# Modulation weights in an adaLN decode block: 128 rows of two terms loaded by four transfers of eight rows

## The chip, the cores and the metric

The kernel runs on one core of one Trainium2 chip. The time is the device time of one execution in microseconds (us); lower is better. The core has five engines, each with an instruction stream of its own: TensorE (PE in the profile, with PEld for its weight loads), VectorE (DVE), ScalarE (ACT), GpSimd (POOL) and SyncE (SP). Data moves between HBM and the on-chip memory SBUF through 16 DMA engines. A transfer is issued as one instruction, here nearly always by SP, and its parts run on several DMA engines side by side. SBUF has 128 partitions; a tile is a number of partitions by a number of bytes in each.

## The reference

One decoding step of a transformer block with adaptive layer norm, four sequences (B = 4), width D = 512, float32 throughout:

```
mod = silu(c) @ w_mod                    # c: 4 x 512, w_mod: 512 x (6*512)
sa, ca, ga, sb, cb, gb = mod in six terms of 4 x 512
h = layernorm(x) * (1 + ca) + sa
x = x + ga * attention(h, k_cache, v_cache, wq, wo)   # 32 query heads, 8 KV heads, 4096 keys of 128
h = layernorm(x) * (1 + cb) + sb
x = x + gb * mixer(h, w1, b1, w2, b2)    # 1 -> 1792 -> 1 per channel, GELU between
```

The K and V caches are 4 x 8 heads x 4096 x 128 floats each: 32 pairs (batch, head) of 2 MB of K and 2 MB of V. `w_mod` is 6 MB: six terms of 512 x 512 floats, 1 MB each. The terms are called 0 to 5 here (sa, ca, ga, sb, cb, gb). A term's 512 rows are the contraction; they are laid out as four blocks of 128 rows (k = 0 to 3), one row to a partition.

## The kernel before

All large arrays go through a ring of three SBUF buffers of 32 KB per partition (pool `ring`, tag `kv`). A buffer is filled by one or more transfers issued by SP; SP waits before it issues until the matmuls that read the buffer's former content are done, so the ring sets the order and the earliest time of every load. SP issues in the order of the program text and does not overtake: a transfer that has to wait holds up all later ones. In order: terms 0 and 1 (`wm01`, 2 MB), the small vectors in three transfers of 6, 10 and 112 partitions, `x`, the query weights (two of 4 MB), the first two K blocks (`load_first`), then one transfer of 4 MB per step with the K of pair i+2 and the V of pair i side by side (`load_pair`), and between them the output weights (`load_wo`, four of 2 MB, which stay in SBUF), terms 2 to 4 (`load_wm24`, 3 MB, one ring buffer, issued in step 1 of the main loop) and, close to the end, term 5 (`load_wm5`).

The main loop runs over the pairs 0 to 23. Step i issues the load for pair i+1, computes the scores of pair i+2 (`scores`, L238, eight matmuls of 128x512 that read K), their row maximum (L243), exponentials (L268), the transposes of pair i+1 (L275), the weighted V sums of pair i (`values`, L301) and the output projection (L337) of pair i-1. From step 9 on, the mixer of a finished batch row is worked in beside it (class `Mixer`). Step 2 also computes the modulation terms 2, 3 and 4: `mod(t)` runs 16 matmuls (`modmm`, L223: four row blocks k by four column blocks c), whose stationary operand is `sT8[:, k]`, silu(c) of that row block repeated to 32 columns, and whose moving operand is the term's block `WM[t][:, k, ...]`; the result is copied to `prep` (L614, L616). The last eight pairs follow an order written out by hand (`PLAN`), in which v29.0 or v31.3 stands for a part of the V sums of pair 29 or 31, and the loads of V for pairs 28 to 31 are transfers of their own (`load_v`, L218); that of pair 31 comes in four pieces of 1 MB, 0.5 MB and twice 0.25 MB. The last pair's V sums are L309. After them come the last batch row's residual, layer norm, mixer (L431, L537, L542) and the output.

`silu(c)` is made at the start from 16 columns `cT` of the small vectors: one activation (L119) and four VectorE instructions (L120 to L124), 16 columns wide, the last of them 128.

The lines that the change and the steps of the prediction touch are L54 to L61 (first loads), L119 to L124 (silu), L137 (terms 0 and 1), L190 (`load_pair`), L199 and L200 (`load_wm24`), L206 (`load_wm5`), L218 (`load_v`), L223 (`modmm`), L301 and L309 (V sums).

Of the kernel before, what the change touches and what calls it, by code (L numbers as in the profile page):

```python
# [8 lines left out]
F32 = mybir.dt.float32  # L9
# [6 lines left out]
B, D, HQ, HKV, SK, DH, F = 4, 512, 32, 8, 4096, 128, 1792  # L16
REP = HQ // HKV
NF = F // 128
EPS = 1e-5
P = 128  # L20
NS = B * HKV
NSM = 3 * NF + 16 + 1

# [5 lines left out]


@with_exitstack
def adaln_decode(ctx: ExitStack, tc: tile.TileContext, small, x, wmod, wq, kk, kv, vv, wo, out):
    nc = tc.nc
    pad = ctx.enter_context(tc.tile_pool(name="pad", bufs=1))
    ring = ctx.enter_context(tc.tile_pool(name="ring", bufs=3))
    wos = ctx.enter_context(tc.tile_pool(name="wos", bufs=1))
    cst = ctx.enter_context(tc.tile_pool(name="cst", bufs=1))
    wk = ctx.enter_context(tc.tile_pool(name="wk", bufs=2))  # L40
    up = ctx.enter_context(tc.tile_pool(name="up", bufs=3))
# [5 lines left out]
    mm = nc.tensor.matmul  # L47
    dv = nc.vector

    neg1 = pad.tile([1, 96], F32, name="neg1")[:, 0:1]  # L50
    sm = cst.tile([P, NSM], F32, name="sm")
    xr = wk.tile([P, D], F32, name="xr", tag="yw", bufs=1)[0:B]
    wm01 = ring.tile([P, 2, 4, D], F32, name="wm01", tag="kv")
    nc.sync.dma_start(wm01, wmod[0])  # L54
    for lo, hi in ((0, 6), (6, 16), (16, P)):
        nc.sync.dma_start(sm[lo:hi], small[lo:hi])
    nc.sync.dma_start(xr, x)
# [1 line left out]
    for k in range(0, 4, 2):  # L59
        t = ring.tile([P, 2, HQ * DH], F32, name=f"wq{k}", tag="kv")  # L60
        nc.sync.dma_start(t, wq[k // 2])  # L61
        wqt += [t[:, 0], t[:, 1]]
    w1, b1, w2 = sm[:, 0:NF], sm[:, NF:2 * NF], sm[:, 2 * NF:3 * NF]
    cT = sm[:, 3 * NF:3 * NF + 16]
    b2 = sm[:, 3 * NF + 16:]

    ident = cst.tile([P, P], F32, name="ident")
    make_identity(nc, ident)
# [25 lines left out]
    wo_t = [wo_p[h // 2][:, h % 2] for h in range(HKV)]  # L94
    prep = cst.tile([P, 4, P], F32, name="prep")
    osb = cst.tile([P, B, P], F32, name="osb")
    sT8 = cst.tile([P, 4, B, 8], F32, name="sT8")

    def rsqrt(ve, n, tag, beside=None, out=None, times=None):
        y = wk.tile([n, 1], F32, name="y" + tag)  # L100
# [11 lines left out]
        if times is not None:  # L112
# [2 lines left out]
        dv.scalar_tensor_tensor(y, q, RS3, y, op0=OP.add, op1=OP.mult)  # L115
        return y

    sg = cst.tile([P, 16], F32, name="sg")
    nc.scalar.activation(sg, cT, AF.Exp, scale=-1.0)  # L119
    dv.tensor_scalar(sg, sg, 1.0, None, op0=OP.add)  # L120
    dv.reciprocal(sg, sg)
    sT = cst.tile([P, 4, B], F32, name="sT")
    dv.tensor_mul(sT.rearrange("p k b -> p (k b)"), sg, cT)  # L123
    dv.tensor_copy(sT8.rearrange("p k b r -> p (k b) r"),  # L124
                   sT.rearrange("p k b -> p (k b)").unsqueeze(2).to_broadcast([P, 16, 8]))

    st = wk.tile([B, 6], F32, name="st0")
    dv.bn_stats(st, xr)
# [34 lines left out]
    rows = cst.tile([B, B, 8], F32, name="rows")  # L163
# [7 lines left out]
    KT, VT, WM = {}, {}, {}  # L171

    def slots():
        return ring.tile([P, 2, SK], F32, name="kv", tag="kv")
# [20 lines left out]
        nc.sync.dma_start(wo_p[h // 2], wo[h // 2])  # L195

    def load_wm24():
        w = ring.tile([P, 3, 4, D], F32, name="wm24", tag="kv")
        nc.sync.dma_start(w[:, 0:2], wmod[1])  # L199
        nc.sync.dma_start(w[:, 2], wmod[2][:, 0])  # L200
        for e in range(3):
            WM[2 + e] = w[:, e]

    def load_wm5():
        t = slots().rearrange("p s (k n) -> p (s k) n", n=D)
        nc.sync.dma_start(t[:, 0:4], wmod[2][:, 1])  # L206
        WM[5] = t[:, 0:4]
        return t[:, 4:6]

    def load_key(t, i):  # L210
# [6 lines left out]
        for lo, hi in zip(cuts, cuts[1:]):  # L217
            nc.sync.dma_start(VT[i][:, lo:hi], src[:, lo:hi])  # L218

    def modmm(pm, t, ks=range(4)):  # L220
        for k in ks:
            for c in range(4):
                mm(pm[32 * c:32 * c + 32, :], sT8[:, k].rearrange("p b r -> p (b r)"),  # L223
                   WM[t][:, k, c * P:(c + 1) * P], start=(k == 0), stop=(k == 3))

    def mod(t):
        pm = ps_e.tile([P, P], F32, name=f"pm{t}", tag="e")
        modmm(pm, t)
        return pm
# [348 lines left out]
    for i in range(NS - HKV):  # L578
# [3 lines left out]
        if i == 1:  # L582
            load_wm24()
# [25 lines left out]
        if i == 2:  # L609
            for t in range(2, 5):  # L610
                pm = mod(t)
# [32 lines left out]
    for step in PLAN.split():  # L644
        op, k = step.rstrip("0123456789."), step.lstrip("abcdefghijklmnopqrstuvwxyzABCDEFGHIJKLMNOPQRSTUVWXYZ")
        i, q = (int(n) for n in (k + ".0").split(".")[:2]) if k else (0, 0)
# [19 lines left out]
        elif op == "LV":  # L666
            load_v(slot[:, i % 2], i, cuts.get(i, (0, 32)))
        elif op == "LW":
            spare = load_wm5()
        elif op == "x":  # L670
            mix.expand(spare if mix.n == 6 else None)
        elif op == "f":
            fold_gate(gate, gates[:1])
            del gates[:1]
        elif step == "T":
            nc.scalar.activation(tab, neg1, AF.Exp)
        elif op == "Y":
            pgx = ps_s.tile([P, 8, P], F32, name="pgx", tag="s")
        elif op == "y":
            pc = fold_groups(ps_m, ACC.pop(B - 1), "m")  # L680
        elif op == "E":
            ep = cst.tile([P, P], F32, name="ep")
            residual(ep, pc)
        elif op == "I":
            mm(pgx[:, 4], ident, ep, start=False, stop=False)
        elif step == "T2":
            nc.scalar.activation(tab, neg1, AF.Abs_reciprocal_sqrt)
        elif step == "T3":
            nc.scalar.activation(tab, neg1, AF.Gelu_apprx_tanh)
        elif op == "zs":  # L690
            row.st = stats(pgx[:, 4], B - 1)
        elif op == "zx":
            dv.tensor_copy(XK[:, B - 1], pgx[:, 4])
        elif op == "zw":
            modmm(pgx[:, 0], 5, (0,) if i == 0 else (1, 2, 3))
        elif op == "zb":
            if i == 0:
                py = ps_s.tile([P, 8, P], F32, name="py3", tag="s")
            row.spread(py[:, 4:], (2 * i, 2 * i + 1))
# [35 lines left out]
```

## Time and profile before

| | us |
|---|---|
| median of 3 runs | 389.47 (389.02 to 390.22) |
| span of the profiled execution, first to last instruction | 386.9 |
| DMA queue of SP (q1), share of 16 engines' span | 94.8% |
| PE busy (weight loads apart) | 298.9 |
| VectorE busy | 215.2 |
| ScalarE busy | 108.0 |
| bytes read from HBM | 157.32 MB |

The profiled execution's own time is its span, 386.9 us, and what lies around it before the first and after the last instruction; the runs' median is 2.6 us above the span. A row of the timeline gives the start, the duration, the engine, the line, the operation, the tiles written and read, and in brackets the idle time before it with what ended it. In the answer by windows, each stretch has its busy time per engine, the granted TensorE clock, the mean busy share of the 16 DMA engines (a share of 0.5 is eight engines at work on average) and GB/s. A share slightly above 1 comes from packets that overlap at their edges or reach over the edge of the window.

### The profile page before, as it was taken

How to read it: one execution, taken by the hardware profiler on the slowest of the kernel's cores; microseconds unless marked ns; L12 is line 12 of the kernel's file. 1: busy time of each engine (PE TensorE's matmuls, PEld its weight loads, DVE VectorE, ACT ScalarE, POOL GpSimd, SP SyncE). 2: the span in 40 equal slices, each digit the busy share in tenths (PEclk: the TensorE clock that was granted, in tenths of full speed). 3: DMA queues.
4: the chain of work that ended last, by engine and by line, in shares of the span. 5: the costliest groups of instructions: out<-in, count | busy, mean ns of one | idle time of the engine just before them, and what ended most of it. 6: DMA issues, size and time to landing. Idle time of an engine off the chain costs nothing.

```text
span 386.9 us, 5714 instructions
## 1 busy us (share of the span) xinstructions
PE 298.9 (77%) x2416; PEld 122.4 (32%) x2416; DVE 215.2 (56%) x516; ACT 108.0 (28%) x132; POOL 0.7 (0%) x6
## 2 busy tenths in 40 slices
PE   0765575863966949979888859999988887999984
PEld 0111121231323313334222323443323342444562
DVE  0420351620542524676766644676875579788766
ACT  0101120110110110113567210213783104757356
POOL 0000000000000000000000000000000000000000
PEclk9998875986695775989999985978999998899999
DMA  8999999999999999999999999999999999999910
GB/s 329 430 434 434 415 451 430 410 449 432 418 447 434 430 434 432 434 432 434 426 434 429 434 429 434 434 432 434 425 434 432 434 429 434 422 427 423 404 46 3
DMA packets 7281, 157.70 MB, mean 408 GB/s; under 512 B 964, under 2 KB 980, under 8 KB 1368
## 3 DMA queue, kind: packets, MB, share of 16 engines
q1 hardware_dynamic: 7248, 157.33, 94.8%
q8 instruction: 19, 0.31, 0.3%
q14 instruction: 6, 0.05, 0.0%
q10 hardware_dynamic: 8, 0.00, 0.0%
HBM read 157.32 MB, written 0.01 MB: 407 GB/s over the span
## 4 chain that ended last, share of the span: by engine, by line
DMA 54%; PE 28%; DVE 16%; issue 1%; SPq 1%; ACTq 0%; DVEq 0%
DMA kv<-in_kv 47%; PE s L238 8%; PE pv L301 7%; DMA wq<-in_wq 6%; DVE m L243 3%; DVE p L275 3%; PE pt L324 2%; PE pa L337 2%; PE pb L258 2%; DVE uu L431 1%; DVE mx L252 1%; DVE acc L353 1%; PE qs L152 1%; PE phb L417 1%; PE pve L309 1%
## 5 line engine op out<-in xcount | busy, mean ns | idle before, releaser
L238 PE MATMUL s<-kv,QT 128*32 128x512 f32 x512 | 76.2, 715 | 35.6 <-DMA kv<-in_kv 32.6
L268 ACT ACTIVATE p<-s,nm 128x1024 f32<-128x1024 f32 x32 | 35.6, 1114 | 199.0 <-DVE nm L263 198.9
L243 DVE TENSOR_REDUCE m<-s 128x1 f32<-128x1024 f32 x32 | 39.2, 1224 | 76.1 <-PE s L238 76.0
L301 PE MATMUL pv<-kv,p 128*32 128x512 f32 x496 | 75.0, 684 | 0.4 <-DMA kv<-in_kv 0.4
L275 DVE STREAM_TRANSPOSE p<-p 128x512 f32<-128x512 f32 x64 | 41.9, 687 | 1.7 <-ACT p L268 1.7
L324 PEld LDWEIGHTS pt<-sel,po 128*128 128x128 f32 x250 | 33.6, 208 | 28.7 <-issue 15.6
L238 PEld LDWEIGHTS s<-kv,QT 128*32 128x32 f32 x512 | 16.3, 125 | 81.3 <-DMA kv<-in_kv 45.3
L337 PE MATMUL pa<-wo,oT 128*32 128x512 f32 x240 | 35.3, 663 | 4.3 <-DVE oT L329 4.2
L324 PE MATMUL pt<-sel,po 128*128 128x4 f32 x250 | 36.2, 268 | 1.4 <-DVE po L315 1.4
L315 DVE COPY po<-pv 128x512 f32<-128x512 f32 x31 | 21.4, 689 | 17.0 <-PE pv L301 17.0
L252 DVE TENSOR_REDUCE mx<-pm 1x128 f32<-1x512 f32 x32 | 21.4, 671 | 0.8 <-PE pm L247 0.7
L258 PEld LDWEIGHTS pb<-neg,mx 1*128 1x128 f32 x64 | 10.8, 210 | 32.9 <-DVE mx L252 31.1
L487 ACT ACTIVATE u<-u 128x1024 f32<-128x1024 f32 x20 | 20.4, 1052 | 2.7 <-DVE u L431 2.6
L431 DVE TENSOR_SCALAR u<-hb,wr,sm 128x512 f32<-128x512 f32 x40 | 19.9, 541 | 1.0 <-PE py L442 0.9
L353 DVE TENSOR_TENSOR acc<-acc,pa 128x512 f32<-128x512 f32 x26 | 17.7, 681 | 3.6 <-PE pa L337 3.6
L268 ACT ACT_TABLE_LOAD x11 | 14.1, 1283 | 19.0 <-DVE nm L263 18.9
L137 PE MATMUL s<-wm,sT 128*4 128x512 f32 x16 | 8.4, 684 | 12.2 <-DVE sT L123 12.2
L258 PE MATMUL pb<-neg,mx 1*128 1x1 f32 x64 | 13.5, 278 | 5.3 <-DVE mx L252 5.3
L487 ACT ACT_TABLE_LOAD x13 | 16.7, 1283 | 0.2
L247 PE MATMUL pm<-ident,m 128*1 128x128 f32 x32 | 9.1, 286 | 9.8 <-DVE rl L284 3.8
L301 PEld LDWEIGHTS pv<-kv,p 128*32 128x32 f32 x496 | 14.1, 146 | 8.1 <-issue 2.1
L247 PEld LDWEIGHTS pm<-ident,m 128*1 128x1 f32 x32 | 2.5, 80 | 39.1 <-DVE rl L284 21.0
(144 smaller groups left out, 212.3 us busy)
## 6 DMA issues: line engine op xcount, KB each, us to landing
kv<-in_kv SPq DMA_DIRECT2D x28, 4096.0 KB, 20.8
wq<-in_wq SPq DMA_DIRECT2D x2, 4096.0 KB
wo<-in_wo SPq DMA_DIRECT2D x4, 2048.0 KB
kv<-in_kv SPq DMA_DIRECT2D x4, 2048.0 KB, 18.5
wm<-in_wmod SPq DMA_DIRECT2D x2, 2048.0 KB
kv<-in_kk SPq DMA_DIRECT2D x1, 4096.0 KB
kv<-in_vv SPq DMA_DIRECT2D x3, 1024.0 KB
wm<-in_wmod SPq DMA_DIRECT2D x1, 1024.0 KB
```

What stands on the lines that cost most here:

```text
L238: mm(s[32 * c:32 * c + 32, n * 512:(n + 1) * 512], QT[:, b, h, :], KT[i][:, (n * 4 + c) * 512:(n * 4 + c + 1) * 512], start=True, stop=True)
L243: dv.tensor_reduce(M[i], S[i], axis=AX.X, op=OP.max)
L252: dv.tensor_reduce(mx, M[i].rearrange("o (c r) -> o r c", c=4).unsqueeze(1).to_broadcast([1, 4, 32, 4]), axis=AX.X, op=OP.max)
L258: mm(pb, M[i].rearrange("o c r -> o (c r)"), neg1, start=True, stop=True)
L268: nc.scalar.activation(p, S[i], AF.Exp, bias=M.pop(i), accum_out=l)
L275: dv.transpose(p, p)
L301: mm(PV[i][32 * q:32 * q + 32, :], pT[:, 128 * k:128 * k + 128:4], VT[i][:, 4 * k:4 * k + 4, :].rearrange("p j d -> p (j d)"), start=(k < ...
L324: mm(pt, po[:, c * DH:(c + 1) * DH], sel[:, c, :], start=(c == 0), stop=(c == n - 1))
L337: mm(pa[32 * g:32 * g + 32, :], oT[:, g:g + 1].to_broadcast([P, 32]), wo_t[h][:, g, :], start=True, stop=True)
L353: dv.tensor_add(ACC[b], ACC[b], pa)
L431: dv.tensor_scalar(u[:, e, :], hb, wr[:, j:j + 1], b1[:, j:j + 1], op0=OP.mult, op1=OP.add)
L487: nc.scalar.activation(u, u, AF.Gelu_apprx_tanh)
```

## The change

The 3 MB of terms 2 to 4 are split in another way. Of terms 2 and 3, the row blocks k = 0 to 2 (384 rows) come as before onto 128 partitions, in one transfer of 12 KB per partition. The last 128 rows (block k = 3) of these two terms are cut into 32 rows of 16 KB, each of which holds four consecutive weight rows of both terms; they land on partitions 0 to 31, in four transfers of eight rows each: transfer e writes partitions e, e+4, ..., e+28. Term 4 leaves the ring buffer: its four row blocks come in two transfers of 512 KB into two buffers of the pool `up`, which the mixer uses later. Term 5's source becomes an array of its own.

Since the last 128 rows now lie as 32 partitions by 4, their product takes four matmul groups with a contraction of 32 rows (q = 0 to 3) in place of one with 128, so terms 2 and 3 have seven groups of four matmuls each in place of four. Their stationary operand is silu(c) in the matching order, which comes as 16 further columns of the small vectors (`NSM` grows from 59 to 75 floats per partition); `sg`, `sT` and `sT8` are twice as wide.

```diff
-NSM = 3 * NF + 16 + 1
+NSM = 3 * NF + 32 + 1
...
-    cT = sm[:, 3 * NF:3 * NF + 16]
-    b2 = sm[:, 3 * NF + 16:]
+    cT = sm[:, 3 * NF:3 * NF + 32]
+    b2 = sm[:, 3 * NF + 32:]
...
-    sT8 = cst.tile([P, 4, B, 8], F32, name="sT8")
+    sT8 = cst.tile([P, 8, B, 8], F32, name="sT8")
...
-    sg = cst.tile([P, 16], F32, name="sg")
+    sg = cst.tile([P, 32], F32, name="sg")
...
     def load_wm24():
-        w = ring.tile([P, 3, 4, D], F32, name="wm24", tag="kv")
-        nc.sync.dma_start(w[:, 0:2], wmod[1])
-        nc.sync.dma_start(w[:, 2], wmod[2][:, 0])
-        for e in range(3):
-            WM[2 + e] = w[:, e]
+        w = ring.tile([P, 7, 2, D], F32, name="wm24", tag="kv")
+        nc.sync.dma_start(w[:, 0:3], w23)
+        for e in range(4):
+            nc.sync.dma_start(w[e:32:4, 3:7], wlow[e])
+        for t in range(2):
+            WM[2 + t] = [(P, k, w[:, k, t]) for k in range(3)] + [(32, 4 + q, w[0:32, 3 + q, t]) for q in range(4)]
+        WM[4] = []
+        for h in range(2):
+            u = up.tile([P, 2, D], F32, name="u")
+            nc.sync.dma_start(u, w4[h])
+            WM[4] += [(P, 2 * h + k, u[:, k]) for k in range(2)]
...
     def load_wm5():
         t = slots().rearrange("p s (k n) -> p (s k) n", n=D)
-        nc.sync.dma_start(t[:, 0:4], wmod[2][:, 1])
-        WM[5] = t[:, 0:4]
+        nc.sync.dma_start(t[:, 0:4], w5)
+        WM[5] = [(P, k, t[:, k]) for k in range(4)]
         return t[:, 4:6]
...
-    def modmm(pm, t, ks=range(4)):
-        for k in ks:
+    def modmm(pm, t, ks=None):
+        n = len(WM[t])
+        for e in range(n) if ks is None else ks:
+            rows, k, w = WM[t][e]
             for c in range(4):
-                mm(pm[32 * c:32 * c + 32, :], sT8[:, k].rearrange("p b r -> p (b r)"),
-                   WM[t][:, k, c * P:(c + 1) * P], start=(k == 0), stop=(k == 3))
+                mm(pm[32 * c:32 * c + 32, :], sT8[0:rows, k].rearrange("p b r -> p (b r)"),
+                   w[:, c * P:(c + 1) * P], start=(e == 0), stop=(e == n - 1))
...
+    w = a["w_mod"].reshape(4, P, 6, D)
...
-        "wmod": con(a["w_mod"].reshape(4, P, 3, 2, D).transpose(2, 1, 3, 0, 4)),
+        "w01": con(w[:, :, 0:2].transpose(1, 2, 0, 3)),
+        "w23": con(w[0:3, :, 2:4].transpose(1, 0, 2, 3)),
+        "wlow": con(w[3, :, 2:4].reshape(4, 8, 4, 2, D).transpose(2, 1, 0, 3, 4)),
+        "w4": con(w[:, :, 4].reshape(2, 2, P, D).transpose(0, 2, 1, 3)),
+        "w5": con(w[:, :, 5].transpose(1, 0, 2)),
```

More of the change, by code (lines that the diff above doesn't have):

```diff
@@ L33, in adaln_decode @@
 @with_exitstack
-def adaln_decode(ctx: ExitStack, tc: tile.TileContext, small, x, wmod, wq, kk, kv, vv, wo, out):
+def adaln_decode(ctx: ExitStack, tc: tile.TileContext, small, x, w01, w23, wlow, w4, w5, wq, kk, kv, vv, wo, out):
     nc = tc.nc
@@ L53, in adaln_decode @@
     wm01 = ring.tile([P, 2, 4, D], F32, name="wm01", tag="kv")
-    nc.sync.dma_start(wm01, wmod[0])
+    nc.sync.dma_start(wm01, w01)
     for lo, hi in ((0, 6), (6, 16), (16, P)):
@@ L121, in adaln_decode @@
     dv.reciprocal(sg, sg)
-    sT = cst.tile([P, 4, B], F32, name="sT")
+    sT = cst.tile([P, 8, B], F32, name="sT")
     dv.tensor_mul(sT.rearrange("p k b -> p (k b)"), sg, cT)
     dv.tensor_copy(sT8.rearrange("p k b r -> p (k b) r"),
-                   sT.rearrange("p k b -> p (k b)").unsqueeze(2).to_broadcast([P, 16, 8]))
+                   sT.rearrange("p k b -> p (k b)").unsqueeze(2).to_broadcast([P, 32, 8]))
     st = wk.tile([B, 6], F32, name="st0")
@@ L710 @@
     cT = a["c"].reshape(B, 4, P).transpose(2, 1, 0).reshape(P, 16)
+    cL = a["c"].reshape(B, 16, 32)[:, 12:].transpose(2, 1, 0).reshape(32, 16)
     small = _np.concatenate([
-        a["B_w1"].reshape(P, NF), a["B_b1"].reshape(P, NF), a["B_w2"].reshape(P, NF), cT,
+        a["B_w1"].reshape(P, NF), a["B_b1"].reshape(P, NF), a["B_w2"].reshape(P, NF), cT, _np.tile(cL, (4, 1)),
         _np.broadcast_to(a["B_b2"].reshape(1, 1), (P, 1))], axis=1)
```

## The prediction

> **What bounds the kernel now.** I read the page's slices of the span first, then its chain, the answer by windows, and the timeline around the changed lines and the end. The slices: the DMA row is at 9 from the second slice until the last two, at 415 to 451 GB/s, while PE, DVE and ACT rise and fall.
>
> ```profile
> DMA  8999999999999999999999999999999999999910
> GB/s 329 430 434 434 415 451 430 410 449 432 418 447 434 430 434 432 434 432 434 426 434 429 434 429 434 434 432 434 425 434 432 434 429 434 422 427 423 404 46 3
> ...
> DMA 54%; PE 28%; DVE 16%; issue 1%; SPq 1%; ACTq 0%; DVEq 0%
> ```
>
> The third line is the chain's share by engine: more than half of what ended last is DMA. The chain in order of time (start, duration, what) shows where DMA gives way to computing for good:
>
> ```profile
> 336.33 21.56 DMA kv<-in_kv
> ...
> 358.03 1.95 PE pv L301 x16
> 359.98 0.86 PE pa L337 x8
> ...
> 367.75 0.42 PE pve L309 x8
> 368.17 0.87 PE pgx L342 x32
> ...
> 384.06 0.29 DVE osb L552
> ```
>
> So the V of pair 29, issued at 336.33, lands at 357.9, and from 358.03 on PE and DVE run to the end without a pause. The timeline at that point and at the last V sums has the waits (in brackets, idle time and releaser):
>
> ```profile
> 358.03 1.95 PE L301 MATMUL pv<-kv,p 128*32 128x512 f32 x16 [0.19 <-DMA kv<-in_kv]
> ...
> 367.10 0.16 PEld L309 LDWEIGHTS pve<-kv,p 128*32 128x32 f32 x8 [0.17 <-DMA kv<-in_vv]
> ...
> 367.74 0.16 PEld L309 LDWEIGHTS pve<-kv,p 128*32 128x32 f32 x8 [0.26 <-DMA kv<-in_vv]
> ```
>
> PE waits for data each time, but only 0.17 to 0.26 us: stream and computing arrive nearly together. A later landing is paid in full from 358.03 on; an earlier one gains at most these waits, 0.19 + 0.17 + 0.26, or about 0.6 us.
>
> The stream itself never pauses, and its end is ragged:
>
> ```profile
> 10.00:30.00 20.00, 14.22 (x72) 3.32 (x76) 6.33 (x21) 0.68 (x2) 0.00 (x0) 1.00 1.01 437
> ...
> 100.00:200.00 100.00, 82.60 (x544) 30.93 (x543) 55.79 (x130) 20.02 (x27) 0.00 (x0) 0.83 1.01 433
> ...
> 366.00:366.50 0.50, 0.50 (x28) 0.50 (x24) 0.50 (x2) 0.32 (x1) 0.00 (x0) 1.00 1.02 410
> 366.50:367.00 0.50, 0.50 (x28) 0.43 (x16) 0.50 (x3) 0.50 (x1) 0.00 (x0) 1.00 0.91 369
> 367.00:367.50 0.50, 0.50 (x24) 0.38 (x16) 0.41 (x1) 0.48 (x2) 0.00 (x0) 1.00 0.60 246
> 367.50:368.00 0.50, 0.50 (x23) 0.26 (x15) 0.19 (x1) 0.50 (x1) 0.00 (x0) 1.00 0.62 262
> 368.00:368.50 0.50, 0.50 (x28) 0.50 (x21) 0.47 (x3) 0.50 (x1) 0.00 (x0) 1.00 0.50 213
> 368.50:369.00 0.50, 0.50 (x21) 0.30 (x13) 0.13 (x1) 0.24 (x2) 0.00 (x0) 1.00 0.58 246
> 369.00:369.50 0.50, 0.50 (x8) 0.49 (x4) 0.11 (x1) 0.00 (x0) 0.00 (x0) 1.00 0.43 164
> 369.50:370.00 0.50, 0.50 (x18) 0.39 (x20) 0.05 (x1) 0.00 (x0) 0.00 (x0) 1.00 0.04 16
> ```
>
> The last two columns are the share of the 16 DMA engines and GB/s. Full until 366.5, then 0.50 to 0.62 for two microseconds, then nothing. 0.5 to 0.6 of 16 is eight to ten engines: about seven have run out of work near 366.8, about nine are two to three microseconds behind, and every transfer is complete only with its slowest engine. No transfer was uneven, all large ones have 128 rows; the lag has grown over the run. The records under these views say it more exactly: each transfer raises its semaphore once per engine. For the last transfer (term 5) the sixteen rises stand at these distances in us from the first, and the small transfers of the start have as many rises as rows:
>
> ```
> term 5, 128 rows, first at 366.64:  0 .30 .43 .74 .77 .84 1.00 2.75 2.79 2.95 3.12 3.17 3.20 3.25 3.39 3.52
> small vectors, 6 rows: 6 rises;  10 rows: 10 rises;  x, 4 rows: 4 rises;  112 and 128 rows: 16 rises
> ```
>
> Seven early, nine late. Single engines fall back when an instruction fetch cuts in; this is their traffic:
>
> ```profile
> q8 instruction: 19, 0.31, 0.3%
> q14 instruction: 6, 0.05, 0.0%
> ```
>
> **The change, part by part.** *Bytes by engine.* Nothing is added to the stream: 3 MB before, 1.5 + 0.5 + 1 MB after. But the 0.5 MB goes in transfers of eight rows. By the counts of rises above (4, 6 and 10 rows on as many engines), eight rows run on eight engines, one row of 16 KB each, so four transfers give eight engines 64 KB each and the other eight nothing; spread evenly it was 32 KB on each of 16. Eight engines carry 32 KB more, eight carry 32 KB less. At 433 GB/s over 16 engines, one moves 27.1 GB/s, so 32 KB are 1.21 us. Since the stream never pauses, this shift stays until its end at about 366.
>
> What that does to the last landing depends on whose load grows. Seven engines are early, and eight get more: at least one late one is among them. The late nine stand within 0.8 us (2.75 to 3.52), so the last landing moves by at least 1.21 - 0.77 = 0.44 us and at most by 1.21; an earlier end is excluded as long as the lags are as they are. I take 1.21, because following the packets one by one back to the start, the slowest engine of all is one of the four that carried a row of `x`. The row sets nest (four engines in the six, six in the ten), and I take it that a set of eight lies between, with those four in it.
>
> [...]
>
> *More transfers.* Seven in place of two. On the eight engines that is five more completions, and term 4 moves in pieces of 4 KB instead of 8 KB. No view prices a completion in a full stream; below it is nothing, above it 0.35 us, an issue row, for five of them if engines waited for SP, which they don't as work is queued. The nearest row is the busy share of 1.01 across transfers (10 to 30 us holds three): no gap at all. I take 0.05.
>
> *SP.* The five more issues cost 0.28 to 0.43 us each by these rows, about 1.8 us more, in a stretch from 59.6 to 72.06 in which SP waits for a ring buffer:
>
> ```profile
> 58.80 0.33 SPq L199 DMA_DIRECT2D wm<-in_wmod  x1
> 59.18 0.43 SPq L200 DMA_DIRECT2D wm<-in_wmod  x1
> 72.06 8.50 SPq L190 DMA_DIRECT2D kv<-in_kv  x2
> ...
> kv<-in_kv SPq DMA_DIRECT2D x28, 4096.0 KB, 20.8
> ```
>
> The last line is the issue list: 20.8 us from issue to landing against 9.7 us that 4 MB take at 433 GB/s, so some 11 us of work are always queued. Nothing is delayed. The two `up` buffers are free then (one of three was used, in the first 25 us).
>
> *PE.* Terms 2 and 3 have 28 matmuls each for 16, in rows 56 for 32:
>
> ```profile
> 82.77 1.62 PE L223 MATMUL pm<-wm,sT 128*32 128x128 f32 x32 [2.59 <-DMA wm<-in_wmod]
> ...
> 84.78 1.93 PE L223 MATMUL pm<-wm,sT 128*32 128x128 f32 x32 [0.40 <-DVE prep L616]
> ...
> 87.13 1.08 PE L223 MATMUL pm<-wm,sT 128*32 128x128 f32 x32 [0.42 <-DVE prep L616]
> ...
> 88.27 17.71 SPq L190 DMA_DIRECT2D kv<-in_kv  x2
> ...
> 94.85 3.64 PE L238 MATMUL s<-kv,QT 128*32 128x512 f32 x16 [6.64 <-DMA kv<-in_kv]
> ```
>
> 24/32 x (1.62 + 1.93) = 2.7 us more if 32 contraction rows cost as much as 128, nothing less than 1.6 (24/32 x 2 x 1.08). Cover: the 6.64 us that PE waits for the next K at 94.85. The ring buffer is released when term 3 is done, not term 4: 88.27 - 1.08 - 0.42 + 2.7 plus up to 1.21 for the landing, so at 89.5 to 90.7 in place of 88.27; with 11 us queued, no engine runs dry.
>
> *Start.* silu(c) on 32 columns instead of 16 and a copy of 256 instead of 128 per partition. The rows there:
>
> ```profile
> 10.47 0.22 ACT L119 ACTIVATE sg<-sm 128x16 f32<-128x16 f32 x1
> ...
> 11.63 0.25 DVE L121 RECIPROCAL sg<-sg 128x16 f32<-128x16 f32 x1
> ...
> 12.13 0.23 DVE L124 COPY sT<-sT 128x128 f32<-128x128 f32 x1
> ...
> 28.17 3.64 PE L152 MATMUL qs<-wq,hT 128*32 128x512 f32 x32 [0.95 <-DMA wq<-in_wq]
> ```
>
> If four small instructions grew by half of 0.25 each, PE would start 0.5 us later; 0.95 us of wait at 28.17 covers it. The copy is beside PE's first matmuls. Nothing.
>
> **The sum:** 1.21 + 0.05 = +1.26 us on the span of 386.9, which makes 388.2. The median of the runs is 389.47, 2.6 above that span; on it, 390.7.
>
> **Rivals.** (a) *Part of it.* The eight engines hold some late ones but not the slowest: +0.44 to +1.0 us, 389.9 to 390.5. For it: the late nine stand close together. Against: the slowest one's packets.
>
> (b) *The eight rows are sprayed evenly*, each 16 KB row in halves over 16 engines. Then the change does not do what its eight rows suggest, and only small costs are left: 0 to 0.1 us, 389.5. Against it the 4, 6 and 10 rises; for it, that those rows were 2 KB and less.
>
> (c) *Not slower: the fetches move.* PE executes 96 more rows (48 matmuls, 48 weight loads) before the long part of the run, so each later fetch on q8 comes earlier, and a fetch that falls on another engine changes who is late. If the late nine become engines that lost 32 KB, all but one, the end comes earlier by up to 1.21 us, of which the tail can take 0.6: 388.9. It decides when the slowest engine's lag falls from 3.5 to under 2.3 us. Against it: 19 fetches on q8 and nine late engines, close together, look like a fixed rotation that hits the same ones again, not chance.
>
> (d) *Each short transfer costs a start-up of its own.* With one row per engine there is nothing to overlap the start of the next with. The nearest row is an issue, 0.28 to 0.43 us: four of them are 1.1 to 1.7 us on top, 391.8 to 392.4. Against: no gap of the busy share anywhere, the early transfers of 6, 10 and 112 rows included.
>
> [...]
>
> **How the numbers follow.** Chances: the forecast 0.55, (a) 0.15, (b) 0.10, (c) 0.12, (d) 0.08. A measurement of this kernel can tell about 0.3% from no change, 1.17 us, since the three runs shown lie 1.2 us apart. The forecast of +1.26 stands just above that bound: with an uncertainty of some 0.3 us I give it about four in five to come out as slower, (d) all, (a) a third; that makes slower 0.57. Faster needs more than the 0.6 us of the tail's waits, a part of (c) and a shift of the median: 0.09. The rest, 0.34, is within the bound. The range from 389.2 to 391.7 takes in (a), (b) and the forecast, and leaves out (c) and (d). The likeliest case's own range is 390.3 to 391.2.
>
> **What would show each step.** Right: in the changed kernel's answer by windows the DMA share stays full until about 366, and its ragged end is longer, from under 366 to about 371, with fewer engines at work in the last microsecond; the chain enters PE at L301 (pair 29) near 359.2 instead of 358.03, with a DMA landing ahead of it, and everything after is shifted by the same 1.2 us; the wait before L238 near 95 is shorter by PE's extra 1.6 to 2.7 us, and is still there. Wrong: the share drops later and all at once (the eight engines were the early ones or the fetches moved); PE near 358 waits no longer than before; idle DMA shares near 76 to 86 us, where the new transfers run (d); L238 near 95 without a wait, which would put PE's extra work on the path.

## The result, and the profile after

The changed kernel takes 391.48 us (median of 8 runs, 390.92 to 394.36); the kernel before, timed beside it, 389.65 (388.97 to 390.22). The ratio is 1.0059 with an interval of 1.0043 to 1.0075: slower, by some 2.3 us (1.7 to 2.9). The medians lie only 1.83 us apart; the ratio is near that of the means, and two of the eight executions of the changed kernel, 392.68 and 394.36, lift its mean. The profiled span is 389.7 us against 386.9, so 2.8 longer. Lines from L223 on moved down by 8 (L223 is L231 now, L238 L246, L301 L309, L309 L317, L337 L345).

The page of the changed kernel, its slices and the chain's share by engine:

```profile
PEclk9998655975595778999999999869999999799899
DMA  8999999999999999999999999999999999999800
GB/s 328 434 431 429 425 436 428 426 433 432 431 439 427 436 434 441 429 441 432 431 426 434 429 431 432 431 431 426 434 429 431 436 431 429 425 428 420 336 5 3
...
DMA 53%; PE 28%; DVE 16%; issue 1%; SPq 1%; ACT 1%; ACTq 0%; DVEq 0%
```

The DMA row is as before: full from the second slice on, with no hole near 80 us (slices 8 and 9), where the new transfers run. The chain in order of time (start, duration, what):

```profile
338.03 21.43 DMA kv<-in_kv
359.46 0.14 issue
359.60 3.32 PE pv L309 x16
362.92 1.19 PE pa L345 x8
...
386.84 0.29 DVE osb L560
```

The V of pair 29 lands at 359.46; before it was 336.33 + 21.56 = 357.89. That is +1.57. The next line is the surprise: the sixteen matmuls of its V sums take 3.32 us where they took 1.95. The answer by windows shows why (its last three columns are the granted clock, the DMA share and GB/s):

```profile
355.60:359.40 3.80, 3.80 (x43) 2.45 (x39) 2.88 (x8) 2.67 (x5) 0.00 (x0) 1.00 0.98 410
359.40:362.80 3.40, 3.22 (x21) 1.25 (x24) 1.67 (x5) 1.74 (x2) 0.00 (x0) 0.59 1.01 426
362.80:366.20 3.40, 3.40 (x32) 1.58 (x27) 1.76 (x4) 0.00 (x0) 0.00 (x0) 0.91 1.00 408
...
367.00:367.50 0.50, 0.50 (x8) 0.00 (x0) 0.46 (x1) 0.00 (x0) 0.00 (x0) 1.00 0.90 377
367.50:368.00 0.50, 0.50 (x6) 0.21 (x2) 0.50 (x2) 0.00 (x0) 0.00 (x0) 1.00 0.77 320
368.00:368.50 0.50, 0.50 (x7) 0.50 (x6) 0.50 (x2) 0.00 (x0) 0.00 (x0) 1.00 0.47 193
...
369.00:369.50 0.50, 0.50 (x28) 0.50 (x24) 0.50 (x2) 0.23 (x1) 0.00 (x0) 1.00 0.15 66
369.50:370.00 0.50, 0.50 (x28) 0.50 (x20) 0.50 (x3) 0.50 (x1) 0.00 (x0) 1.00 0.23 98
370.00:370.50 0.50, 0.50 (x28) 0.50 (x24) 0.50 (x1) 0.48 (x2) 0.00 (x0) 1.00 0.12 49
```

For one stretch of 3.41 us right after the landing, from 360.03 to 363.45, TensorE was granted half its clock (0.50 there, 0.59 and 0.91 in windows that don't lie exactly on it). In both traces the clock is either full or half, in stretches that last 3.41 us or a whole multiple of it (where the record's end does not cut one short), and their bounds lie at other times in each. In the profile of before the window from 359.40 to 362.80 has the full clock:

```profile
359.40:362.80 3.40, 3.40 (x34) 1.46 (x26) 1.80 (x5) 0.18 (x1) 0.00 (x0) 1.00 0.99 414
```

So the 2.8 us between the two profiles are 1.57 of later landing and some 1.2 of a slow stretch of PE. The ragged end (from 367.00 on) is longer: shares of 0.12 to 0.23, two to four engines of 16, were still at work between 369.0 and 370.5, where before the stream was over at 369.5.

The rises of the semaphore, one for each engine, say what the new transfers did. Each of the four transfers of eight rows raised its semaphore eight times. These are distances in us from the first rise, for a 4 MB load ahead of the new transfers and for the first 4 MB load behind them, from the records under the views:

```
before,  ahead,  first at 70.84:  0 .03 .07 .26 .30 .35 .37 .42 .47 .51 .51 .69 .84 .92 1.17 1.84
before,  behind, first at 92.69:  0 .03 .07 .30 .34 .38 .42 .47 .50 .51 .83 .93 1.07 1.75 1.79 2.11
changed, ahead,  first at 70.66:  0 .36 .37 .39 .43 .50 .51 .62 .66 .71 .77 .78 .78 .85 1.62 1.75
changed, behind, first at 91.78:  0 .03 .16 .22 .26 .39 .45 1.35 2.50 2.60 2.77 2.82 2.84 3.56 3.61 4.01
```

In the changed kernel the sixteen engines fall into eight and eight, with over 1.1 us of nothing between them (1.35 to 2.50). Followed one by one, the packets of eight engines move back by 2.45 us against those of the other eight: twice 1.21, and some 0.02 us more; four packets of 16 KB, at 0.61 us each, make the same.

Around the changed work, the timeline of the changed kernel (idle time and releaser in brackets; SPq rows are issues):

```profile
28.02 3.64 PE L152 MATMUL qs<-wq,hT 128*32 128x512 f32 x32 [0.67 <-DMA wq<-in_wq]
...
61.66 2.82 SPq L201 DMA_DIRECT2D wm<-in_wlow  x4
64.52 8.24 SPq L207 DMA_DIRECT2D u<-in_w  x2
77.32 3.98 SPq L190 DMA_DIRECT2D kv<-in_kv  x2
...
83.32 1.76 PE L231 MATMUL pm<-wm,sT 32*32 32x128 f32 x32 [1.50 <-DMA wm<-in_wlow]
85.47 3.37 PE L231 MATMUL pm<-wm,sT 128*32 128x128 f32 x56 [0.39 <-DVE prep L624]
...
88.90 0.33 SPq L190 DMA_DIRECT2D kv<-in_kv  x1
...
95.84 1.94 PE L246 MATMUL s<-kv,QT 128*32 128x512 f32 x8 [4.65 <-DMA kv<-in_kv]
```

PE's longer terms ate 2.0 us of the wait before the next K (6.64 before, 4.65 now), the ring buffer came free at 88.90 instead of 88.27, and the start used 0.28 of its 0.95 us. All of that is covered. What is new is SP: between the two transfers of term 4 it waits for an earlier load to land, and then again before the next load, which is issued at 77.32 instead of 72.06. The view of waits (us in total, times, longest) names the releases:

```profile
SPq L207 <- DMA kv<-in_kv: 7.5, 1, 7.5
...
SPq L190 <- DMA wo<-in_wo: 4.5, 1, 4.5
```

### The profile page after: what moved, and what is told of

It is laid out like the page before. It is cut to its first block, busy times and chain, and to the rows that moved or that the text cites. A ratio compares the mean times of both kernels' runs of the same rounds, so it can differ in the third digit from the quotient of the medians.

```text
span 389.7 us, 5819 instructions
## 1 busy us (share of the span) xinstructions
PE 299.7 (77%) x2464; PEld 122.6 (31%) x2464; DVE 215.2 (55%) x516; ACT 108.0 (28%) x132; POOL 0.7 (0%) x6
## 4 chain that ended last, share of the span: by engine, by line
DMA 53%; PE 28%; DVE 16%; issue 1%; SPq 1%; ACT 1%; ACTq 0%; DVEq 0%
DMA kv<-in_kv 41%; PE s L246 9%; PE pv L309 7%; DMA wm<-in_wlow 5%; DMA kv<-in_kk 5%; DVE m L251 4%; DVE p L283 2%; PE s L137 2%; PE pt L332 2%; DMA sm<-in_small 2%; DVE mx L260 2%; PE pa L345 2%; DVE uu L439 1%; PE pm L231 1%; PE pb L266 1%; DVE acc L361 1%
## 5 line engine op out<-in xcount | busy, mean ns | idle before, releaser
L246 PE MATMUL s<-kv,QT 128*32 128x512 f32 x512 | 76.8, 721 | 39.3 <-DMA kv<-in_kv 34.6
L309 PE MATMUL pv<-kv,p 128*32 128x512 f32 x496 | 73.8, 675 | 0.2 <-DMA kv<-in_kv 0.2
L246 PEld LDWEIGHTS s<-kv,QT 128*32 128x32 f32 x512 | 15.8, 123 | 84.1 <-DMA kv<-in_kv 50.5
L345 PE MATMUL pa<-wo,oT 128*32 128x512 f32 x240 | 34.9, 654 | 4.2 <-DVE oT L337 4.1
L309 PEld LDWEIGHTS pv<-kv,p 128*32 128x32 f32 x496 | 14.4, 147 | 8.2 <-issue 3.4
```

Of the source, the lines that this page charges most:

```text
L246: mm(s[32 * c:32 * c + 32, n * 512:(n + 1) * 512], QT[:, b, h, :], KT[i][:, (n * 4 + c) * 512:(n * 4 + c + 1) * 512], start=True, stop=True)
L309: mm(PV[i][32 * q:32 * q + 32, :], pT[:, 128 * k:128 * k + 128:4], VT[i][:, 4 * k:4 * k + 4, :].rearrange("p j d -> p (j d)"), start=(k < ...
L345: mm(pa[32 * g:32 * g + 32, :], oT[:, g:g + 1].to_broadcast([P, 32]), wo_t[h][:, g, :], start=True, stop=True)
```

## The experiments

**The late landing comes from the four short transfers.** First the changed kernel again, and, on the same chip, the changed kernel with only the short transfers undone: the fourth row block lies on 128 partitions again and comes with the others in one transfer, while the arrays of the other terms, term 4 in the two `up` buffers and the wider silu stay.

```diff
-        w = ring.tile([P, 7, 2, D], F32, name="wm24", tag="kv")
-        nc.sync.dma_start(w[:, 0:3], w23)
-        for e in range(4):
-            nc.sync.dma_start(w[e:32:4, 3:7], wlow[e])
+        w = ring.tile([P, 4, 2, D], F32, name="wm24", tag="kv")
+        nc.sync.dma_start(w, w23)
...
-            WM[2 + t] = [(P, k, w[:, k, t]) for k in range(3)] + [(32, 4 + q, w[0:32, 3 + q, t]) for q in range(4)]
+            WM[2 + t] = [(P, k, w[:, k, t]) for k in range(4)]
```

> The changed kernel, unaltered, a second profile. Three things were found in its first profile: the V of pair 29 landed 1.57 us later than before, 1.26 us of it from the 32 KB more on eight engines, some 0.3 us from where the slowest engine stood after the first 10 us, and a stretch of 3.4 us at half clock at 360.0 that cost some 1.3 us. Theory L (lag): the part of 1.2 us is there again, the part of the start differs by a few tenths, the half clock at the end comes or stays away with the phase of its windows. Then the time is +1.2 to +1.6 us without it and +2.5 to +2.9 with it, the median +1.5 to +2.3. Rival H (half clock as a fixed cost of the change): it comes again in the same place and the median is +2.5 or more.

> As the changed kernel, but the fourth row block of terms 2 and 3 comes with the others on 128 partitions, one transfer of 16 KB per partition, and its product is one group of four matmuls again. Term 4 in two pieces of its own, the wider silu and the wider small vectors stay. Theory L: the time of before within 0.4 us, and the slowest engine's lag at the end like before, 3.3 to 3.8 us. Rival R, if it is the start or term 4's pieces: +1 us or more stays.

The changed kernel again: 391.26 us against 389.45, ratio 1.0040 (1.0020 to 1.0061). With the short transfers undone: 389.47, ratio 0.9996 (0.9978 to 1.0014). Within that interval, from 0.9 us faster to 0.5 us slower, nothing of the cost is left. The chain of the first has the late landing without the slow stretch, on a span of 388.4:

```profile
337.11 22.32 DMA kv<-in_kv
359.43 0.14 issue
359.57 1.95 PE pv L309 x16
```

In the second, span 387.2, the V sums of pair 29 start where they did in the kernel before (timeline):

```profile
358.22 1.95 PE L307 MATMUL pv<-kv,p 128*32 128x512 f32 x16 [0.18 <-DMA kv<-in_kv]
```

So the late landing comes with the short transfers, and the slow stretch of PE isn't tied to it.

**Sixteen rows instead of eight.** Two transfers of 16 rows, onto every second of the partitions 0 to 31. If sixteen rows go to as many engines, as four, six, eight and ten rows did by their rises, each engine carries one row, and none carries more than another.

```diff
-        for e in range(4):
-            nc.sync.dma_start(w[e:32:4, 3:7], wlow[e])
+        for e in range(2):
+            nc.sync.dma_start(w[e:32:2, 3:7], wlow[e])
...
-        "wlow": con(w[3, :, 2:4].reshape(4, 8, 4, 2, D).transpose(2, 1, 0, 3, 4)),
+        "wlow": con(w[3, :, 2:4].reshape(4, 16, 2, 2, D).transpose(2, 1, 0, 3, 4)),
```

> As the changed kernel, but the same 32 rows of 16 KB come in two transfers of 16 rows (partitions e, e+2, ..., e+30) in place of four of eight. Everything behind the load is the same: 28 matmuls per term, wider silu, term 4 in pieces. Theory L: sixteen engines take one row each per transfer, 32 KB per engine, no lag is added, the time is that of before within 0.5 us. Rival R (the rest of the change costs the time: PE's longer terms, the start, more transfers): the time stays at +1.8 us or more. Rival P (partitions 0 to 31 are a bottleneck of their own): the two transfers take twice as long on all 16 engines, every landing is 1.2 us later, the time is +1.2 to +1.8 us.

393.66 us, ratio 1.0095 (1.0069 to 1.0121): slower than the change itself and than any of the three theories said, and V of pair 29 lands at 361.30. The windows where the two transfers run:

```profile
78.00:80.00 2.00, 1.71 (x13) 0.45 (x17) 1.96 (x6) 0.00 (x0) 0.00 (x0) 1.00 1.19 393
80.00:82.00 2.00, 1.84 (x18) 0.51 (x10) 0.91 (x3) 0.53 (x1) 0.00 (x0) 1.00 0.86 162
82.00:84.00 2.00, 1.07 (x28) 0.59 (x24) 0.69 (x1) 0.68 (x2) 0.00 (x0) 1.00 1.01 219
```

The engines count as busy (0.86 and 1.01) but move only 162 and 219 GB/s: 30 of the 32 rows of 16 KB take 0.9 to 1.5 us here instead of 0.61, and packets of 12 KB of the transfer ahead that run beside them are slow too (up to 1.1 us; 0.46 in the changed kernel). The engines disturb each other, and the landing is about 3 us later. This run can't tell whether an even load would have cost nothing, since another cost took its place; it shows that busy engines are not moving engines, and that share and GB/s have to be read together. In the changed kernel eight rows four partitions apart ran at 0.61 us each, undisturbed, onto the same partitions 0 to 31, so these are not a bottleneck in every placement. The "twice as long" of rival P was an estimate of mine; the rows took 1.5 to 2.5 times as long, and the landing came 3.2 us later than in the kernel with 128 rows (361.30 against 358.09). What in the placement makes it was not shown.

**How much, and onto which engines.** Three times the kernel before with an extra load that nothing reads, into the free quarter of the ring buffer: 32 KB each onto the first four engines, onto eight engines, and onto all sixteen.

```diff
-        w = ring.tile([P, 3, 4, D], F32, name="wm24", tag="kv")
+        w = ring.tile([P, 4, 4, D], F32, name="wm24", tag="kv")
...
+        for e in range(4):
+            nc.sync.dma_start(w[e:16:4, 3], wmod[2][e:16:4, 1])        # four rows, 4 x 32 KB in all
...
+        for e in range(4):
+            nc.sync.dma_start(w[e:32:4, 3], wmod[2][e:32:4, 1])        # eight rows, 8 x 32 KB in all
...
+        nc.sync.dma_start(w[:, 3, 0:2], wmod[2][:, 1, 0:2])            # 128 rows, 16 x 32 KB in all
```

> The kernel before, with four further transfers of four rows of 8 KB into the unused part of the buffer of terms 2 to 4 (bytes that nothing reads): 128 KB in all, 32 KB on each of four engines. Theory L, with the slowest engine among the first four: the last landings come 1.2 us later although only 0.13 MB of 157 are added; +1.2 us, or up to +2.5 with a stretch at half clock. Rival A (the slowest engine is not among the four): +0 to +0.4 us. Rival E (time goes by bytes): 128 KB at 433 GB/s, +0.3 us.

> The kernel before, with four further transfers of eight rows of 8 KB into the unused part of the buffer of terms 2 to 4 (bytes that nothing reads): 256 KB, 32 KB on each of eight engines, and nothing taken from the other eight. Theory L (only the slowest engine counts): as the changed kernel and as the four-row transfers, the V of pair 29 lands at 359.2 to 359.5, +1.2 us; that the other eight have less to do in the changed kernel is worth nothing. Rival S (the spread between engines costs by itself, so a smaller one costs less): below +0.8 us.

> The kernel before, with one further transfer of 512 KB on 128 partitions in the same place, 32 KB on each of 16 engines (bytes that nothing reads). Theory L: the same +1.2 us as 128 KB on four engines and 256 KB on eight, V of pair 29 at 359.2 to 359.5. Rival S: less than those two, since no engine falls behind the others.

| extra load | bytes | median, before beside it | ratio | V of pair 29 lands | span |
|---|---|---|---|---|---|
| four engines | 128 KB | 390.24, 389.45 | 1.0018 (1.0000 to 1.0036) | 359.40 | 388.4 |
| eight engines | 256 KB | 390.36, 389.08 | 1.0029 (1.0013 to 1.0045) | 359.16 | 388.2 |
| sixteen engines | 512 KB | 390.93, 389.08 | 1.0052 (1.0032 to 1.0072) | 359.21 | 388.4 |

128, 256 and 512 KB delay the landing by about the same, 1.3 to 1.5 us against 357.89 in the first profile of before, and 1.1 to 1.4 against 358.02 in its second. For the landing it is not the bytes that count but the 32 KB on the slowest engine, and this engine is one of the first four, since these alone suffice. Counted from the slowest engine's own first long packet to the landing, the time is 350.12 us in the kernel before, 351.38 with four engines loaded and 351.40 in the changed kernel: the term of the sum measures 1.28. The landings differ by a few tenths more because this engine stands at 7.8 to 8.1 us at its start, from execution to execution.

The times are less clear than the landings. The medians rise with the bytes, by 0.8, 1.3 and 1.9 us, and for four engines the interval reaches down to no change at all. The fastest executions of the three lie close together (390.01, 389.92 and 390.14, against 388.77 and 388.68 of the kernel before beside them); why more of the slower ones fell to the sixteen engines was not followed. And only with eight engines does PE wait for the landing. The V sums of pair 29 with eight engines and, below, with four:

```profile
359.30 1.95 PE L303 MATMUL pv<-kv,p 128*32 128x512 f32 x16 [0.20 <-DMA kv<-in_kv]
```

```profile
359.77 1.96 PE L303 MATMUL pv<-kv,p 128*32 128x512 f32 x16
```

With four engines PE comes to them 0.37 us after the landing (359.40), without a wait, and with sixteen 0.33 us after it. In both profiles PE was held up before: its granted clock between 309 and 315 us is 0.72, where it is 1.00 in both profiles of the kernel before and in the one with eight engines. So their spans of 388.4 can't be put down to the landing alone.

**The clock.** The kernel before against itself, and the changed kernel twice more:

> The kernel before against itself, with a second profile. Theory L: the slowest engine's start differs between executions by a few tenths (its first large packet after the small vectors stood at 7.77 us in the first profile of before, at 7.93 to 8.16 in five others), so the V of pair 29 lands between 357.9 and 358.2 and the span is 386.9 to 387.3 without a stretch at half clock near the end. The ratio is 1.000 within 0.002; if it is further away, differences of half a microsecond between the other runs mean nothing.

> The changed kernel, a third profile, in the call with the even and uneven additions. Theory L: V of pair 29 at 359.3 to 359.6; span 388.3 to 388.6, or 389.5 to 390 if a stretch at half clock falls behind 355; median +1.2 to +1.8, within 0.5 us of the two runs with additions.

> The changed kernel once more beside them. Theory L and C: times in two groups, near 390.2 to 390.6 and 391.3 to 391.8, V of pair 29 landing at 359.2 to 359.6; median +1.3 to +2.4 by how the groups fill.

The kernel before: 390.02 us beside 389.08, ratio 1.0012 (0.9998 to 1.0026). This time its profile has the slow stretch too, on a span of 388.3 instead of 386.9, although V of pair 29 lands at 358.02, as early as ever. Its windows and the V sums in its timeline:

```profile
355.00:358.30 3.30, 3.12 (x42) 2.33 (x38) 2.25 (x8) 2.14 (x3) 0.00 (x0) 1.00 1.01 429
358.30:361.70 3.40, 3.40 (x20) 1.15 (x22) 1.43 (x4) 1.41 (x2) 0.00 (x0) 0.50 0.99 413
```

```profile
358.15 3.61 PE L301 MATMUL pv<-kv,p 128*32 128x512 f32 x16 [0.18 <-DMA kv<-in_kv]
```

So the half clock is not the change's doing alone: it hits executions of either kernel. From the landing of V 29 to the end of the span it is 29.0 us without it (386.9 - 357.89; 388.4 - 359.43 in the repeat) and 30.2 to 30.3 with it (388.3 - 358.02; 389.7 - 359.46). The times fit that: 109 executions of the kernel before fall into a group around 389.0 (67 of them, cut at 389.75) and one above it, most of it around 390.2 (42); 44 of the changed kernel into one around 390.4 (19, cut at 391.1) and one above it, most of it around 391.5 (25). At the upper end of each lies a third, smaller group, at 391.5 to 392.2 (8 of the 42) and at 392.7 to 394.4 (5 of the 25). That the slow stretch after the landing makes the second group rests on one profile of each kernel. Each group is shifted by about 1.4 us: about 1.2 of it in the span (by the medians of the groups, 387.2, 388.3 and 389.9 before, where 101 of the 109 spans are on record, and 388.4, 389.6 and 391.0 in the changed kernel), and 0.2 outside it, before its first or after its last instruction (1.8 us before, 2.0 in the changed kernel). These 0.2 us are not the short transfers' doing: with 128 rows in their place it is 2.0 us as well. Where more of the changed kernel's executions than of the other's fall into the upper groups, mean and median shift by more than 1.4.

The changed kernel twice more: 391.39 beside 389.08, ratio 1.0040 (1.0024 to 1.0056), and 390.52 beside 389.43, 1.0028 (1.0011 to 1.0045). Both medians missed what was expected (+2.3 where +1.2 to +1.8 was, +1.1 where +1.3 to +2.4 was): how the groups fill moves a median by half a microsecond and more. In the first the profile fell on an execution of the third group (span 391.0): PE came to the V sums of pair 29 only at 360.96, 1.74 us after their V had landed, and then ran them at half clock. In the second (span 388.3) it came to them 0.38 us after the landing, without a wait. Both have the half clock between 309 and 315 us too (0.72). So the landing sets the time only where PE is not held up more by its clock.

**Taking the slow stretch away.** If half clock follows a stretch of thin matmuls (42 in the 3.30 us ahead of it in the second profile of the kernel before), denser work for PE in that stretch should end it in both kernels, and what remains between them should be the landing alone. Three 128x512 matmuls whose result nothing reads stand before the transposes of pair 30:

```diff
-    v28.1 b31 l30 B31 e31 LV31 V28 L30 c t30.1 a28 l31 L31 v29.0 t31.1 v29.1 A28 p28 t30.0 V29 a29 v30.0
+    v28.1 b31 l30 B31 e31 LV31 V28 L30 c w t30.1 a28 l31 L31 v29.0 t31.1 v29.1 A28 p28 t30.0 V29 a29 v30.0
...
+        elif op == "w":
+            fil = ps_s.tile([P, 1024], F32, name="fil", tag="s")
+            for _ in range(3):
+                mm(fil[0:32, 0:512], QT[:, 0, 0, :], wo_t[0][:, 0, :], start=True, stop=True)
```

> The kernel before, with three further matmuls of 128x512 between the mixer's (after L30) and the output projection of pair 28, into a PSUM tile that nothing reads; they put work into the stretch of thin matmuls ahead of the V sums of pair 29, after which the clock was halved in three of ten profiles, of the kernel before too. They take 1.3 us of PE time. Theory C (thin matmuls in one window of 3.4 us bring the half clock, and it makes the second group of times, 1.2 us above the first): the second group becomes rare, so the times lie within 0.6 us of each other apart from single ones, and no profile has half clock between 345 and 370; the median is +0 to +1.3 us. Rival N (the second group has another cause): the times stay in two groups 1.2 us apart, both raised by what the matmuls cost.

> The changed kernel with the same three matmuls. Theory C: with the half clock gone from both, the difference to the kernel before with the three matmuls is the lag alone, 1.2 to 1.4 us, where without them the medians differ by 1.8 to 2.3. Rival D (the change costs PE time besides the lag): the difference stays at 1.8 us or more.

Before with the filling: 390.71 us, ratio 1.0021 (1.0000 to 1.0042); changed with the filling: 392.26, ratio 1.0067 (1.0044 to 1.0091). All times of the first lie within 0.9 us (390.57 to 391.43), of the second within 1.05 (391.97 to 393.02): apart from three single executions they lie within 0.6, as expected, and the groups 1.2 us apart are gone in both. The granted clock is 1.00 where the slow stretch was in each profile. Filling costs more than the half clock did (390.7 against the lower group's 389.0): the matmuls take 2.55 us, where 1.3 were expected, and lie on PE's path now, so the chain goes over to PE with the load that lands before it. The chains of the two, kernel before first:

```profile
335.15 18.04 DMA kv<-in_kv
...
356.75 2.55 PE fil L673 x6
...
360.51 1.88 PE pv L301 x16
```

```profile
335.65 18.84 DMA kv<-in_kv
...
358.05 2.56 PE fil L681 x6
...
361.81 1.88 PE pv L309 x16
```

The landings, of the V of pair 28, are at 353.19 and 354.49, and the V sums of pair 29 start at 360.51 and 361.81: 1.30 apart each time, and so are the spans, 388.9 and 390.2. With the clock out of the way the change costs 1.3 us inside the span. The medians differ by 1.55; the rest, 0.25, lies outside the span (1.78 and 2.03 in the two profiled executions), as found above for all executions. What in the change makes it was not followed.

## Why the prediction was right or wrong

The direction held. The median, 391.48, lies in the range of 389.2 to 391.7, but above the likeliest case's own 390.3 to 391.2; and the ratio, put on the 389.47 that the forecast started from, makes 391.8, just above the range. The size did not hold: +1.26 us stands against 2.3 (1.7 to 2.9) in the first comparison, and against ratios of 1.0028 to 1.0040, 1.1 to 1.6 us, in the three repeats. That the repeats lie around the forecast is in part luck, since it lacked two terms, and the groups filled differently each time.

*Bytes by engine: right.* Eight rows ran on eight engines, and the slowest engine, one of the four that carried a row of `x`, is among them. Predicted 1.21 + 0.05, measured 1.28. The eight rises of each short transfer and the sixteen in eight and eight give the count. The trace does not number the engines.

*More transfers, PE, start: right.* No dip of the DMA share near 80 us; PE's terms 2 and 3 grew by some 2.4 us (0.86 + 1.76 + 3.37 in place of 1.62 + 1.93, where the 0.86 is the first 24 instructions of term 2; all but these at a clock of 0.50 to 0.62, before and after) inside a wait of 6.64; the start kept 0.67 us of its wait.

*SP: harmless, but not for the reason given.* Nothing was delayed, I said, because queue and buffers were free. SP did wait 7.5 us and then 4.5 us for earlier loads to land, and the next load was issued 5.3 us late. The 11 us of queued work hid it.

*The ragged end: its end right, its beginning wrong.* The last rise of term 5 came at 371.70, as forecast (about 371), but the share stayed full until 367.0 instead of falling before 366: of the early engines some got 32 KB more and of the late ones some 32 KB less, and they met in the middle. Term 5's rises are two at 366.1 to 366.3, eleven from 368.1 to 369.0 and three from 370.5 to 371.7, where before there were seven early and nine late ones.

*The failed step: the sum, with "from 358.03 on PE and DVE run to the end without a pause" under it.* No pause, but not one speed. The sum was the lag alone and had no term for a stretch of half clock on PE, worth 1.2 us, that strikes part of the executions of both kernels. The profile of before fell on an execution without it, and the median of the runs mixes both kinds, so adding the lag to that median was right only if both kernels are struck equally often. In the first comparison they were not (4 of 8 executions before, 7 of 8 after, by the same cuts), nor over all of them (42 of 109, 25 of 44). Whether the later landing makes the stretch likelier, or this is chance, stays open: the runs made can't tell. By the groups the first comparison's 2.3 us come apart about so (an estimate): 1.4 for the shift of every group, that is the lag and the 0.2 us outside the span, for which the sum had no term either; 0.4 for three more of eight executions in the upper groups; and 0.5 for the two at 392.68 and 394.36, of which no profile was taken.

"A later landing is paid in full" held where PE waits for the V of pair 29, in seven of the profiles without filling. In the four with a half clock between 309 and 315 us PE came to it late by itself.

*Rivals.* (a) is out, as the full 32 KB came through; (b) by the split into eight and eight; (d) by rows of 0.61 us without gaps, although its 391.8 to 392.4 comes nearest to the 391.8 of the ratio: the number would have fitted, for a cause that is not there. (c) is out as well: the fetches did come earlier (the fourth on q8 at 107.32 in place of 113.44), but the lengths of the fetches on q8 (0.88 to 0.97 us up to 360) repeat in a cycle of eight, which begins at another engine in the changed kernel's profile, but also in the second profile of the kernel before; and the landing came later, not earlier.

## What to carry to other kernels

In this stream, which never pauses, transfers of four, six, eight and ten rows raised their semaphores as often as they have rows, so each was a load on as many engines, and a late landing was delayed by what came onto the slowest of them: 128 KB on four engines delayed it by 1.4 us, 512 KB on sixteen by 1.2 (359.40 and 359.21 against 358.02). A short transfer that leaves out the slowest engine was not run; that the load on four more engines added nothing (359.16 against 359.40) speaks for its being free. Find that engine from the rises of a late transfer's semaphore before placing odd pieces, and prefer 128 rows (389.47 us here, against 391.26 with eight); sixteen rows, two partitions apart, were worse than eight (393.66). Where a tail bound by PE begins behind a stretch of thin matmuls, look at the granted clock in more than one profile of the kernel before: a term of 1.2 us that comes and goes is as large as many changes.

## What the runs showed of the hardware

Each instruction fetch of 16 KB on q8 put the engine that it fell on 1.42 us behind, followed packet by packet: 0.88 to 0.96 us for itself, and 0.47 to 0.55 by which the packet behind it took longer. By 360 us there were 16 of them, two on each of eight engines in rotation, while of the six of 8 KB on q14 four came to one of the first four engines, at 0.84 us each (0.55 and 0.59 for the other two). Twice 1.42 is 2.84 and four times 0.84 is 3.36: that is where the nine late engines of the kernel before, 2.75 to 3.52 us behind, come from.

The granted clock is full or half in both traces, never between, and every stretch of one or the other that the records hold to its end lasts 3.41 us or a whole multiple of it (3.41 to 102.4). The stretch behind the landing is one such length, and it begins at 360.03 in the changed kernel's first profile and near 358.3 in the second of the kernel before; in the first profile of the kernel before it is missing, with full clock from 332.33 to the end. It did not come after idle time: PE had been busy 3.12 of the 3.30 us ahead of it, with 42 mostly thin matmuls, and 3.24 of 3.42 us, with 38, in the changed kernel. With three dense matmuls there it came in neither profile. What the clock goes by stays open.

Sixteen rows of 16 KB onto partitions two apart moved at 162 to 219 GB/s (80 to 84 us), where with eight rows four apart it was 403 to 447 and with the extra load on 128 rows 389 to 410, and SP waited 7.5 and 4.5 us for landings when seven transfers were issued close together.
